# Local attention and RWKV channel mix: second query tile loaded and scored in halves, other load order, other product orders

## The chip, the cores and the metric

The kernel runs on one core of one Trainium2 chip. The metric is device time in microseconds: the median of three runs of the whole program. On a core, TensorE (PE) multiplies matrices, VectorE (DVE) and ScalarE (ACT) do the elementwise work, GpSimd (POOL) does a few small things here, and SyncE (SP) issues every DMA of this kernel.

## The reference

```python
# attention: q, k, v of shape (4, 8, 768, 64), 8 memory keys and values per head
for c in range(24):                       # chunks of 32 queries
    k_full = concat(mem_k, k[chunk with 16 to the left, 8 to the right])   # 64 keys
    v_full = concat(mem_v, v[the same])
    s = q[chunk] @ k_full.T / 8
    a = exp(s - max(s)); a = a / (sum(a) + 1e-9)
    out[chunk] = a @ v_full
x = out as (4, 768, 512)
# RWKV channel mix, d_model 512, d_ff 1024
x_prev = x one token earlier (zero at the start of a sequence)
xk = mu_k * x + (1 - mu_k) * x_prev;  xr = mu_r * x + (1 - mu_r) * x_prev
k = maximum(xk @ w_k, 0);  v = (k * k) @ w_v;  r = sigmoid(xr @ w_r)
y = r * v
```

All of it is float32.

## The kernel before

The 3072 tokens are 24 query tiles of 128, two of which make a unit of 256 tokens; twelve units pass through the kernel. For a unit, PE computes the scores (`s`, from one load `qk` for each tile that holds queries and keys together), DVE and ACT make the softmax in `e` (maximum, subtraction, exponential, sum, normalization), and PE multiplies with the values (`px`, from the load `vw`). In the first three units `e` is transposed by PE against the identity `id_sb` (`pt`) and copied to `aTz`. From the fourth unit on DVE transposes it in blocks (`eT`, L900), SP writes that to DRAM (`eD`, L907) and reads it back in four pieces as `aTz` (L911); the rows of `px` go to the columns of `xT` in the same way from the seventh unit on (`xD`, `xT`).

The channel mix of a unit is made of `ph` (first product), `kf` (its relu and square), `pr` (gate product), `sg_sb` (sigmoid) and the second product. For accuracy, operands are split into a high and a low part (`xh`/`xl`, `wk`/`wl`, `ah`/`al`), each product is three matmuls, and the second product of a unit is composed of seven partial products p1 to p7, which collect in the banks `accx` (p1, p2), `accy` (p6, p5, p3) and `accz` (p7, p4). The weights arrive as 64-bit words (`raw`) that ACT (L465) and DVE (a sign mask L470, then a join L474) turn into floats. Units 0 and 1 work while the weights still arrive and use plain float32 matmuls (`xf`, `w`).

A planner in Python lists all operations with costs and lays each on its engine. PE's order is written out by hand: `LEAD` for units 0 and 1 (s scores, t transposes, a attention times values, h first product, g gate, v second product), and for each later unit a list in `STAGES` (h0 to h3 parts of the first product, s or z the scores of two or three units ahead, a, b or x the `px` of one or two units ahead, g the gates of the next unit, p1 to p7 partial products). `LOADS` is the order of the first loads. SP's queue takes one DMA after the other, in the planner's order; an issue that waits holds up all behind it. The others' order follows from the planner's costs, with extra waits named in `FORCE`: "n" makes tile 0's normalization wait for tile 1's subtraction, "j" makes w0's join wait for tile 1's normalization. Warm matmuls, which multiply zeros, are placed in PE's gaps before the first `ph`, to keep its clock up; a row `warm 128x256` of the order is one float32 matmul, which shows as two records in the trace. Tile 0 of unit 0 is loaded and scored in two halves (`first_part`), tile 1 whole (`part`).

Of the kernel before, what the change touches and what calls it, by code (L numbers as in the profile page):

```python
# [16 lines left out]
P = 128  # L17
# [19 lines left out]
FORCE = "njt"  # L37
HALF = 2
LOADS = "q0a q0b q1 id w0 v0 v1 w1a w1b w2 w4 w3 q3 q2 w5 w6 v2 w7 w8 v3 q4 w9 q5"
LEAD = "s0.0.0 s0.0.1 s0.1 t0 t1 a0 a1 h0.0.0 h0.0.1 h0.1.0 h0.2.0 h0.3.0 s1.0 s1.1 h0.3.1 g0.0.0 h0.3.2 g0.1.0 h0.3.3 g0.0.1 t2 g0.1.1 a2 t3 v0.0.0 a3 v0.1.0 s2.0 v0.1.1 h1.0.0 h1.0.1 v0.0.1 h1.0.2 h1.0.3 h1.1.0 h1.1.1 h1.1.2 t4 t5 h1.1.3 a4 a5 g1.0 s3.0 g1.1 v1.0.0 v1.0.1 g2.0 v1.1.0 g2.1 v1.1.1"  # L40
STAGES = {
# [19 lines left out]
FETCH, FETCH_LEAD, FETCH_US, FETCH_AT, FETCH_FROM, FETCH_RATE = 256, 40, 4.9, 123, 2600, (0.0046, 0.0088)  # L61
# [49 lines left out]
class Plan:  # L111
# [22 lines left out]
    def place(self, o, free, held):  # L134
# [14 lines left out]
        for eng, cost, port in o.alts:  # L149
            t = max([free.get(eng, 0.7)] + [e + (SELF if g == eng else HOP)[eng if g == eng else g] for e, g in ready])  # L150
            if eng == "pe":
                cost, _ = self.fetched(t, cost, port)
# [7 lines left out]
    def fetched(self, t, cost, n):  # L160
# [46 lines left out]
    def told(self, done):  # L207
# [56 lines left out]
    def turn(self, goal, ease):  # L264
# [10 lines left out]
        while len(done) < len(self.ops):  # L275
# [69 lines left out]
def local_attention__then__channel_mix(  # L345
# [41 lines left out]
    nc.vector.memset(zero_sb, 0.0)  # L387
    nc.gpsimd.memset(aTz[0:64, 1], 0.0)
# [154 lines left out]
    NG = 2 * QPU * NPAIR  # L543

    def scores(u):
# [24 lines left out]
        def part(c, n, prev, first):  # L570
# [68 lines left out]
            if u == 0 and c == QPU - 1:  # L639
# [3 lines left out]
            return o_s, [o_n] * n  # L643

        def first_part():
            mx, sm, pt = Slot("sm"), Slot("sm"), {}
            R = NPAIR // 2

            def e4(b):
                return T["e", 0].rearrange("p (h c r) k -> p h c r k", h=2, c=QPU)[:, :, 0, R * b : R * (b + 1)]  # L650

            def s4(b, h=None):
                if b == 0:
                    return T["s", 0, h][:, : R * NK].rearrange("p (r k) -> p r k", k=NK)
                return T["s", 0, 2].rearrange("p (h g k) -> p h g k", h=2, k=NK)[:, :, :R]

            def f_s(b):
                if b == 0:
                    for h in range(2):
                        T["s", 0, h] = ps("m", f"s0_0_{h}")  # L660
                        nc.vector.memset(s4(0, h)[0:CHUNK, :, 0:LEFT], NEG)
                    T["s", 0, 2] = ps("s", "s0_0_2", QPU)
                    nc.vector.memset(s4(1)[0:CHUNK, :, :, 0:LEFT], NEG)
                for r in range(R):
                    for j in range(NJ):
                        for h in range(2):
                            q, k = operands(0, R * b + r, j, slice(64 * h, 64 * h + 64))
                            k0 = LEFT if j == 0 else 0
                            o = s4(b, h) if b == 0 else s4(b)[:, h]
                            nc.tensor.matmul(o[CHUNK * j : CHUNK * (j + 1), r, k0:], q, k[:, k0:], start=True, stop=True)  # L670
# [3 lines left out]

            def f_max(b):
                if b == 0:
                    pt["mx"] = sb("sm", [P, 2, NPAIR], "mx0_0")
                    for h in range(2):
                        nc.vector.reduce_max(mxs(0)[:, h], s4(0, h), axis=AX.X)
                else:  # L680
                    nc.vector.reduce_max(mxs(1), s4(1), axis=AX.X)

            def f_sub(b):
                if b == 0:
                    T["e", 0] = sb("e", [P, NG, NK], "e0")
                    for h in range(2):
                        m = mxs(0)[:, h].unsqueeze(2).to_broadcast([P, R, NK])
                        nc.vector.tensor_sub(e4(0)[:, h], s4(0, h), m)
                else:
                    nc.vector.tensor_sub(e4(1), s4(1), mxs(1).unsqueeze(3).to_broadcast([P, 2, R, NK]))  # L690

            def f_exp(b):
                nc.scalar.activation(e4(b), e4(b), AF.Exp, scale=SCALE)

            def f_sum(b):
                if b == 0:
# [1000 lines left out]
```

## Time and profile before

| | |
|---|---|
| median of 3 runs | 376.4 us (376.38 to 376.56) |
| the profiled execution | 376.67 us, span 374.9 us |
| PE busy | 367.7 us, 98% of the span |
| DVE busy | 322.7 us, 86% |
| ACT busy | 206.2 us, 55% |
| DMA | 64.78 MB, mean 173 GB/s |
| granted TensorE clock | 1.00 in every row shown here |

The span is the time from the first to the last instruction of the core; 1.8 us of the profiled execution lie around it. PE's share of the span is high all through, so a change of the time must come out of the few microseconds in which PE is idle, or out of the stretch before its first useful product.

### The profile page before, as it was taken

How to read it: one execution, taken by the hardware profiler on the slowest of the kernel's cores; microseconds unless marked ns; L12 is line 12 of the kernel's file. 1: busy time of each engine (PE TensorE's matmuls, PEld its weight loads, DVE VectorE, ACT ScalarE, POOL GpSimd, SP SyncE). 2: the span in 40 equal slices, each digit the busy share in tenths (PEclk: the TensorE clock that was granted, in tenths of full speed). 3: DMA queues.
4: the chain of work that ended last, by engine and by line, in shares of the span. 5: the costliest groups of instructions: out<-in, count | busy, mean ns of one | idle time of the engine just before them, and what ended most of it. 6: DMA issues, size and time to landing. Idle time of an engine off the chain costs nothing.

```text
span 374.9 us, 11497 instructions
## 1 busy us (share of the span) xinstructions
PE 367.7 (98%) x5084; PEld 339.6 (91%) x5084; DVE 322.7 (86%) x524; ACT 206.2 (55%) x307; POOL 2.4 (1%) x9
## 2 busy tenths in 40 slices
PE   7999999999999999999999999999999999999996
PEld 5886579988999999999999998999999999999996
DVE  3899999999999499989699997996998988788274
ACT  2797996954774386475068157238338244156260
POOL 2000000000000000000000000000000000000000
PEclk9999999999999999999999999999999999999999
DMA  7999981324701735556692485266343340400101
GB/s 287 403 417 409 389 309 71 113 87 140 274 39 72 262 120 179 215 165 240 246 278 93 153 288 179 64 220 230 127 154 115 112 169 2 143 30 0 58 1 58
DMA packets 24146, 64.78 MB, mean 173 GB/s; under 512 B 2720, under 2 KB 10784, under 8 KB 23712
## 3 DMA queue, kind: packets, MB, share of 16 engines
q1 hardware_dynamic: 24096, 64.04, 47.8%
q8 instruction: 40, 0.66, 0.7%
q14 instruction: 10, 0.08, 0.1%
HBM read 49.88 MB, written 14.16 MB: 171 GB/s over the span
## 4 chain that ended last, share of the span: by engine, by line
PE 82%; DMA 9%; DVE 5%; SPq 1%; issue 1%; ACT 0%; DVEq 0%
PE ph L1479 26%; PE pr L1368 14%; PE accy L1270 10%; PE accx L1270 7%; PE accz L1270 6%; PE pv L1581 4%; DMA raw<-in_w_k_dram 4%; PE s L588 4%; PE ph L1454 3%; PE px L771 3%; PE px L843 2%; PE pv L1568 2%; DMA qk<-in_qk_dram 2%; DMA aTz<-eD 1%; DMA xT<-xD 1%
## 5 line engine op out<-in xcount | busy, mean ns | idle before, releaser
L1479 PE MATMUL ph<-xh,wk 128*128 128x256 f32 x320 | 89.1, 278 | 0.0
L1479 PE MATMUL ph<-xh,wl 128*128 128x256 f32 x320 | 88.0, 275 | 0.0
L1479 PE MATMUL ph<-xl,wk 128*128 128x256 f32 x320 | 88.0, 275 | 0.0
L1498 ACT ACTIVATE kf<-ph 128x512 f32<-128x512 f32 x47 | 27.6, 596 | 88.7 <-PE ph L1479 88.4
L1479 PEld LDWEIGHTS ph<-xh,wk 128*128 128x128 f32 x320 | 61.4, 192 | 0.8
L1479 PEld LDWEIGHTS ph<-xh,wl 128*128 128x128 f32 x320 | 61.5, 192 | 0.0
L1479 PEld LDWEIGHTS ph<-xl,wk 128*128 128x128 f32 x320 | 61.4, 192 | 0.0
L1215 DVE TENSOR_TENSOR al<-kf,ah 128x512 fp32r<-128x512 f32 x50 | 33.6, 679 | 1.8 <-PE accz L1270 1.6
L1368 PE MATMUL pr<-wr,xh 128*128 128x512 f32 x88 | 34.1, 388 | 0.0
L1368 PE MATMUL pr<-wr,xl 128*128 128x512 f32 x88 | 33.4, 379 | 0.0
L1368 PE MATMUL pr<-wl,xh 128*128 128x512 f32 x88 | 33.4, 379 | 0.0
L397 ACT CAST ah<-kf 128x512 fp32r<-128x512 f32 x45 | 27.3, 620 | 9.7 <-DVE kf L1193 7.2
L1505 ACT ACTIVATE kf<-kf 128x512 f32<-128x512 f32 x45 | 28.1, 632 | 1.1
L1377 ACT ACTIVATE sg_sb<-pr 128x512 f32<-128x512 f32 x24 | 14.0, 597 | 20.5 <-PE pr L1368 20.3
L1270 PE MATMUL accx<-wv,ah 128*128 128x256 f32 x80 | 22.1, 276 | 0.0
L1270 PE MATMUL accx<-wv,al 128*128 128x256 f32 x80 | 22.0, 275 | 0.0
L1270 PE MATMUL accx<-wl,ah 128*128 128x256 f32 x80 | 22.0, 275 | 0.0
L588 PEld LDWEIGHTS s<-qk 64*32 64x32 f32 x1472 | 15.2, 105 | 4.0 <-issue 2.9
L1368 PEld LDWEIGHTS pr<-wr,xh 128*128 128x128 f32 x88 | 16.7, 189 | 2.5
L1368 PEld LDWEIGHTS pr<-wr,xl 128*128 128x128 f32 x88 | 16.6, 189 | 2.3
L1368 PEld LDWEIGHTS pr<-wl,xh 128*128 128x128 f32 x88 | 16.7, 189 | 1.9
L588 PE MATMUL s<-qk 64*32 64x64 f32 x1472 | 17.2, 225 | 1.1 <-DMA qk<-in_qk_dram 1.1
(165 smaller groups left out, 956.0 us busy)
## 6 DMA issues: line engine op xcount, KB each, us to landing
qk<-in_qk_dram SPq DMA_DIRECT2D x23, 768.0 KB, 6.1
vw<-in_vw_dram SPq DMA_DIRECT2D x24, 512.0 KB, 5.2
out_dram<-o SPq DMA_DIRECT2D x23, 256.0 KB, 2.4
eD<-eT SPq DMA_DIRECT2D x9, 512.0 KB, 2.7
aTz<-eD SPq DMA_DIRECT2D x36, 128.0 KB, 3.0
raw<-in_w_v_dram SPq DMA_DIRECT2D x4, 1024.0 KB, 10.2
raw<-in_w_k_dram SPq DMA_DIRECT2D x3, 1024.0 KB, 10.6
xD<-aTz SPq DMA_DIRECT2D x6, 512.0 KB, 2.6
```

What stands on the lines that cost most here:

```text
L397: e.copy(dst, src)
L588: nc.tensor.matmul(s5[CHUNK * j : CHUNK * (j + 1), h, d - c, r, :], *operands(ts[d], r, j, slice(64 * h, 64 * h + 64)), start=True, stop=True,
L771: nc.tensor.matmul(p3[64 * h : 64 * h + 64, 2 * g : 2 * g + 2, CHUNK * j : CHUNK * j + CHUNK], v[:, g, h, j, :], a[:, h, g, j, :], start=True,
L1215: nc.vector.tensor_sub(low(n), place[n](), T["ah", u, n].bitcast(F32))
L1270: nc.tensor.matmul(o, x, w, start=(n in fresh and c + i == 0), stop=(c == cs[-1] and i == 2), skip_group_check=True)
L1368: nc.tensor.matmul(pairs(p), x[:, place_of(u)[k], c * P : (c + 1) * P], woven(w), start=(k + n == 0), stop=(k == KT - 1 and n == 2),)
L1377: nc.scalar.activation(sg, p, AF.Sigmoid)
L1454: nc.tensor.matmul(pairs(T["ph", u, f][:, i * UTOK : (i + 1) * UTOK]), w[:, fc], x[:, :, k].rearrange("p t n -> p n t"), start=(i + k + n ...
L1479: nc.tensor.matmul(pairs(p[:, i * UTOK : (i + 1) * UTOK]), w[:, fc], x[:, :, place_of(u)[k]].rearrange("p t n -> p n t"), start=(k + n == ...
L1498: e.activation(part(), p, AF.Relu)
L1505: e.activation(q, q, AF.Square)
L1581: nc.tensor.matmul(pairs(p), x[:, tc_], woven(w), start=(f + n == 0), stop=(f == FT - 1 and n == 2),)
```

## The change

The second query tile's `qk` is loaded as two DMAs of 128x768, scored in two halves of 64 matmul calls in all, and its maximum, subtraction, exponential and sum are done by halves. Tile 0's second half of scores goes to two banks of its own. The first value tile `vw` and the first weight chunk w0 are loaded ahead of `id_sb` and `mu_sb`. Of `FORCE` only "t" is left, which keeps a copy on ACT. The lists in `LOADS`, `LEAD` and `STAGES` are other permutations, and the planner's constants for warm matmuls and for PE's instruction fetch are other numbers. The diff cut to its core:

```diff
-FORCE = "njt"
+FORCE = "t"
 HALF = 2
-LOADS = "q0a q0b q1 id w0 v0 v1 w1a w1b w2 w4 w3 q3 q2 w5 w6 v2 w7 w8 v3 q4 w9 q5"
...
+WARM = ((0.2, 1.1), (0.9, 0.3), (0.12, 0.43))
+FUSED, FUSED_US = (), 1.2
+LOADS = "q0a q0b q1a q1b v0 w0 id v1 w1a w1b w2 w4 w3 q2 q3 w5 w6 w7 w8 v2 w9 v3 q4 q5"
...
 STAGES = {
-    0: "z h0 h2 h3 h1 x g0 p1 p7 p6 p2 p5 g1 p3 p4",
...
-    5: "h1 z h0 h2 x h3 p1 g0 p7 p6 g1 p5 p2 p4 p3",
...
+    0: "z h0 h2 h1 h3 x g0 p1 p7 p6 p4 p5 p2 g1 p3",
...
+    5: "z h0 h1 h2 x h3 g0 p1 p7 p6 g1 p2 p5 p4 p3",
...
+        def first_part(t, prev):
...
+            def f_max(b):
+                if b == 0:
+                    pt["mx"] = sb("sm", [P, 2, NPAIR], f"mx0_{t}")
+                heads(b, lambda h, s: nc.vector.reduce_max(mxs(b)[:, h], s, axis=AX.X))
...
+            def f_exp(b):
+                if not fused:
+                    nc.scalar.activation(e4(b), e4(b), AF.Exp, scale=SCALE)
+                    return
...
-            if t == 0:
-                l.append([op(("dma", 1.05), lambda b=b: f_load(0, b), new=[x] * (b == 0), use=[x] * b, due=0.1 * b) for b in range(2)])
-                loads.update(q0a=l[0][0], q0b=l[0][1])
+            if u == 0:
+                l.append([op(("dma", 1.05), lambda b=b, t=t: f_load(t, b), new=[x] * (b == 0), use=[x] * b, due=0.2 * t + 0.1 * b) for b in range(2)])
+                loads.update({f"q{t}a": l[t][0], f"q{t}b": l[t][1]})
...
-                n = 0 if ("ph", 0, 0) in T else int((o.start - busy - 0.2) / (0.43 if busy else 1.1))
+                gap = o.start - busy
+                spare, each = WARM[0] if not busy else WARM[1] if gap > 2 else WARM[2]
+                n = 0 if ("ph", 0, 0) in T else int((gap - spare) / each)
```

What it moves on the engines, at the two places that matter here. First the start of the program on SP, the queue of loads. Before:

```order
L561 DMA qk_86<-in_qk_dram 128x768 x2
L561 DMA qk_134<-in_qk_dram 128x1536
L416 DMA id_sb<-in_ident_dram 128x128
L417 DMA mu_sb<-in_mu_dram 128x8
L445 DMA raw_187<-in_w_k_dram 128x1024
L745 DMA vw_210<-in_vw_dram 128x1024
L745 DMA vw_212<-in_vw_dram 128x1024
L445 DMA raw_214<-in_w_k_dram 128x512 x2
L445 DMA raw_250<-in_w_k_dram 128x1024
L447 DMA sg_sb<-in_w_r_dram 128x2x512
L445 DMA raw_335<-in_w_k_dram 128x1024
```

and of the changed kernel:

```order
L572 DMA qk_87<-in_qk_dram 128x768 x2
L572 DMA qk_138<-in_qk_dram 128x768 x2
L786 DMA vw_183<-in_vw_dram 128x1024
L457 DMA raw_185<-in_w_k_dram 128x1024
L428 DMA id_sb<-in_ident_dram 128x128
L429 DMA mu_sb<-in_mu_dram 128x8
L786 DMA vw_233<-in_vw_dram 128x1024
L457 DMA raw_236<-in_w_k_dram 128x512 x2
L457 DMA raw_318<-in_w_k_dram 128x1024
L459 DMA sg_sb<-in_w_r_dram 128x2x512
L457 DMA raw_345<-in_w_k_dram 128x1024
```

The first `vw` and the first `raw` (w0) now stand ahead of `id_sb` and `mu_sb`; up to the fourth `raw` of 128x1024 the same loads are in the queue. On PE the same start, from the last scores of tile 0 to the first `px`, before:

```order
L1639 MATMUL warm<-zero_sb 128x256 x3
L588 MATMUL s_1_148<-qk_134 32x64 x32
L1639 MATMUL warm<-zero_sb 128x256 x5
L751 MATMUL pt_199<-id_sb,e_136 128x128 x4
L1639 MATMUL warm<-zero_sb 128x256 x3
L751 MATMUL pt_223<-id_sb,e_136 128x128 x4
L771 MATMUL px_232<-aTz,vw_210 64x2x32 x16
L771 MATMUL px_258<-aTz,vw_212 64x2x32 x16
```

and of the changed kernel:

```order
L1682 MATMUL warm<-zero_sb 128x256
L677 MATMUL s_1_146<-qk_138 32x64 x16
L1682 MATMUL warm<-zero_sb 128x256
L677 MATMUL s_1_146<-qk_138 32x64 x16
L1682 MATMUL warm<-zero_sb 128x256 x9
L792 MATMUL pt_220<-id_sb,e_82 128x128 x4
L792 MATMUL pt_228<-id_sb,e_82 128x128 x4
L812 MATMUL px_243<-aTz,vw_183 64x2x32 x16
L812 MATMUL px_266<-aTz,vw_233 64x2x32 x16
```

Tile 1's scores stand in two parts with a warm matmul between, nine warm matmuls follow in place of five, and the three between the two transposes `pt` are gone.

The second place is the stage of unit 5 (o5, with unit 8's softmax e8), on DVE, from the normalization of e8 to its block transpose eT8, before:

```order
L622 TENSOR_TENSOR e8_2667<-e8_2667,sum8_0_2969 128x1024
L1312 TENSOR_TENSOR o5_1_2916<-accz5_2897,o5_1_2916 128x256
L1032 TENSOR_TENSOR xl6_0_3017<-df6_2669,xh6_0_2914 128x1024
L1335 TENSOR_TENSOR o5_1_2916<-o5_1_2916,sg_sb_78 128x512
L1312 TENSOR_TENSOR o5_0_2867<-accy5_2920,o5_0_2867 128x256
L1340 TENSOR_TENSOR o5_0_2867<-accx5_2853,sg_sb_78 128x256
L1342 TENSOR_TENSOR o5_0_2867<-o5_0_2867,sg_sb_78 128x256
L900 STREAM_TRANSPOSE eT8_3204<-e8_2667 128x1024
```

and of the changed kernel:

```order
L633 TENSOR_TENSOR e8_2676<-e8_2676,sum8_0_2931 128x1024
L1256 TENSOR_TENSOR al2_5_2935<-kf5_1_2758,ah3_5_2972 128x512
L1073 TENSOR_TENSOR xl6_0_2989<-df6_2707,xh6_0_2907 128x1024
L1381 TENSOR_TENSOR o5_0_2914<-accx5_2890,sg_sb_78 128x256
L1353 TENSOR_TENSOR o5_1_2937<-accy5_2939,o5_1_2937 128x256
L941 STREAM_TRANSPOSE eT8_3017<-e8_2676 128x1024
```

Between the two, four instructions stand in place of six; the sums of accz and of the last accy, and the gates of o5_1 and o5_0, have gone behind eT8. On SP at the same place, before:

```order
L1315 DMA out_0_dram<-o5_1_2916 128x512
L1315 DMA out_0_dram<-o5_0_2867 128x512
L907 DMA eD8_3206<-eT8_3204 128x1024
L561 DMA qk20_3212<-in_qk_dram 128x1536
L911 DMA aTz_79<-eD8_3206 32x4x256 x4
L561 DMA qk21_3297<-in_qk_dram 128x1536
```

and of the changed kernel:

```order
L948 DMA eD8_3033<-eT8_3017 128x1024
L1356 DMA out_0_dram<-o5_1_2937 128x512
L1356 DMA out_0_dram<-o5_0_2914 128x512
L952 DMA aTz_79<-eD8_3033 32x4x256 x4
L572 DMA qk20_3144<-in_qk_dram 128x1536
L572 DMA qk21_3179<-in_qk_dram 128x1536
```

The write eD8 has moved ahead of the two output stores, and the four reads aTz<-eD8 ahead of both loads of queries and keys.


## Rows read from the trace of the kernel before

**Rows 1.** The view of PE's waits: engine, line, what for; us, times, longest us.

```profile
PE px L843 <- DMA aTz<-eD: 1.2, 2, 0.6
```

**Rows 2.** Busy time of the engines by stretches: length, busy us (instructions), granted clock, DMA share, GB/s.

```profile
16.56:40.00 23.44, 23.33 (x232) 17.20 (x228) 22.71 (x33) 20.52 (x31) 0.00 (x0) 1.00 1.02 412
...
200.00:374.90 174.90, 170.53 (x2187) 164.75 (x2186) 144.09 (x248) 77.97 (x117) 0.00 (x0) 1.00 0.33 113
```

**Rows 3.** Timeline of PE around the stall: start us, duration us, engine, line, operation, tiles, count.

```profile
224.17 0.28 PE L1479 MATMUL ph<-xh,wl 128*128 128x256 f32 x1
...
227.28 0.48 PE L1368 MATMUL pr<-wr,xh 128*128 128x512 f32 x1
```

**Rows 4.** Timeline of PE at the same place one stage later.

```profile
254.16 0.28 PE L1479 MATMUL ph<-xh,wl 128*128 128x256 f32 x1
...
255.78 0.48 PE L1368 MATMUL pr<-wr,xh 128*128 128x512 f32 x1
```

**Rows 5.** Timeline of DVE, 207 to 219 us.

```profile
209.38 1.21 DVE L622 TENSOR_TENSOR e<-e,sum 128x1024 f32<-128x1024 f32 x1
...
212.36 0.68 DVE L1335 TENSOR_TENSOR o<-o,sg_sb 128x512 f32<-128x512 f32 x1
212.96 0.42 DVE L1312 TENSOR_TENSOR o<-accy,o 128x256 f32<-128x256 f32 x1
...
213.96 1.24 DVE L900 STREAM_TRANSPOSE eT<-e 128x1024 f32<-128x1024 f32 x1
```

**Rows 6.** Timeline of SP's queue, 205 to 227 us.

```profile
215.22 0.33 SPq L907 DMA_DIRECT2D eD<-eT  x1
215.60 0.45 SPq L561 DMA_DIRECT2D qk<-in_qk_dram  x1
218.12 2.88 SPq L911 DMA_DIRECT2D aTz<-eD  x4
```

**Rows 7.** DMA issues of the whole run: line by tiles, KB of each, median us to landing.

```profile
vw<-in_vw_dram SPq DMA_DIRECT2D x24, 512.0 KB, 5.2
...
eD<-eT SPq DMA_DIRECT2D x9, 512.0 KB, 2.7
...
raw<-in_w_k_dram SPq DMA_DIRECT2D x3, 1024.0 KB, 10.6
```

**Rows 8.** Timeline of PE at the start.

```profile
1.18 2.93 PE L1639 MATMUL warm<-zero_sb 128*128 128x256 f32 x6 [1.18 <-DVE zero_sb L387]
4.05 0.68 PE L670 MATMUL s<-qk 64*32 64x48 f32 x32
4.98 0.68 PE L670 MATMUL s<-qk 64*32 64x48 f32 x32 [0.25 <-DMA qk<-in_qk_dram]
...
8.64 0.85 PE L588 MATMUL s<-qk 64*32 64x64 f32 x64 [1.08 <-DMA qk<-in_qk_dram]
9.42 2.43 PE L1639 MATMUL warm<-zero_sb 128*128 128x256 f32 x10
...
13.55 0.66 PE L751 MATMUL pt<-id_sb,e 128*128 128x128 f32 x4
...
16.56 2.48 PE L1425 MATMUL ph<-xf,w 128*128 128x128 f32 x17
```

**Rows 9.** Timeline of ACT at the start.

```profile
14.25 1.17 ACT L397 COPY aTz<-pt 64x512 f32<-64x512 f32 x2
```

**Rows 10.** Timeline of DVE at the start.

```profile
13.41 0.69 DVE L470 TENSOR_SCALAR raw<-raw 128x1024 uint32<-128x1024 uint32 x1
14.26 1.23 DVE L474 SCALAR_TENSOR_TENSOR w<-w,raw 128x1024 uint32<-128x1024 uint32 x1
```

**Rows 11.** Timeline of SP's queue, 236 to 256 us.

```profile
242.72 0.34 SPq L907 DMA_DIRECT2D eD<-eT  x1
...
247.77 1.75 SPq L911 DMA_DIRECT2D aTz<-eD  x4
```

**Rows 12.** The tile aTz between 240 and 256 us.

```profile
DMA to landing us min/median/max: 2.6/3.0/4.1
```

More of the change, by code (lines that the diff above doesn't have):

```diff
@@ L151, in place @@
             if eng == "pe":
-                cost, _ = self.fetched(t, cost, port)
+                o.ready = max([0.0] + [e + HOP[g] for e, g in ready if g != "pe"])
+                cost, _ = self.fetched(t, cost, port, o.ready)
             elif port:
@@ L158, in place, with fetched @@
         return best
-    def fetched(self, t, cost, n):
+    def fetched(self, t, cost, n, ready):
         d = self.count - FETCH_FROM
@@ L216, in edge @@
             need[b] += 1
-        follows, prev, waits = {}, {}, {}
+        follows, prev, waits, opened = {}, {}, {}, {}
         for o in done:
@@ L225, in told @@
                     waits[o].update(d for d in h[-n].users if d is not o)
+                if s.tag in opened and opened[s.tag] is not o:
+                    edge(opened[s.tag], o)
+                opened[s.tag] = o
                 h.append(s)
@@ L291, in turn @@
                 o.lone, o.n = o.alts[0][1:]
-                cost, self.marks = self.fetched(t, o.lone, port)
+                cost, self.marks = self.fetched(t, o.lone, port, o.ready)
                 free[eng] = t + cost
@@ L642, in part @@
                         prior[y].deps.append(o)
[L643 to L670, printed above, removed]
-            def mxs(b):
-                return pt["mx"][:, :, R * b : R * (b + 1)]
[L675 to L696, printed above, removed]
-                    pt["sum"] = sb("sm", [P, 2, NPAIR], "sum0_0")
-                sm = pt["sum"]
-                nc.vector.reduce_sum(sm[:, :, R * b : R * (b + 1)], e4(b), axis=AX.X)
-                if b:
-                    nc.vector.tensor_scalar_add(sm, sm, 1e-9)
-                    nc.vector.reciprocal(sm, sm)
-            def f_norm():
-                e = grid(T["e", 0], 0, 1)
-                nc.vector.tensor_mul(e, e, pt["sum"].unsqueeze(3).to_broadcast([P, 2, NPAIR, NK]))
-            o_s = o_b = None
-            es_, banks = [], [[Slot("m"), Slot("m")], [Slot("s")]]
-            for b in range(2):
-                o_s = op(("pe", 0.45, 80 - 16 * b), lambda b=b: f_s(b), [l[0][b], o_s], new=sum(banks, []) if b == 0 else [], use=[qs[0]] + banks[b], due=due["s", 0, 0, b])
-                o_m = op(("dve", 0.36 if b else 0.5), lambda b=b: f_max(b), [o_s, o_b], new=[mx] * (b == 0), use=[mx] + banks[b])
-                o_b = op(("dve", 0.36 if b else 0.5), lambda b=b: f_sub(b), [o_m], new=[es] * (b == 0), use=[mx, es] + banks[b])
-                es_.append(op(("act", 0.36), lambda b=b: f_exp(b), [o_b], use=[es]))
-            o_u = op(("dve", 0.36), lambda: f_sum(0), es_[:1], new=[sm], use=[es])
-            o_u = op(("dve", 0.74), lambda: f_sum(1), [o_u, es_[1]], use=[es, sm])
-            prior.update(norm=op(("dve", 0.63, True), f_norm, [o_u], use=[es, sm]))
-            return o_s, [prior["norm"]]
@@ L720, in scores @@
+            else:
+                prior.update(norm=o_n)
+            return o_s, [o_n]
         qs = [Slot(big("q", t)) for t in ts]
@@ L731, in scores @@
         for c in range(0, QPU, step):
-            o_s, o_n = first_part() if u + c == 0 else part(c, step, o_s, u > 0)
+            o_s, o_n = first_part(c, o_s) if u == 0 else part(c, step, o_s, u > 0)
             done += o_n
@@ L796, in attention @@
         da = due.get(("a", t), 0.0)
-        lv = loads[f"v{t}"] = op(("dma", 1.35), f_loadv, new=[vs], lat=3.3 if u > 3 else DLAT)
+        lv = loads[f"v{t}"] = op(("dma", 2.05 if t == 1 else 1.35), f_loadv, new=[vs], lat=3.3 if u > 3 else DLAT + 0.3 * (t == 1))
         if u >= MOVED:
```

97 lines of the change are left out of this document (91 added, 6 removed), and 10 rows, old and new, of the table STAGES.

## Prediction

> **What bounds the kernel now.** I first read PE's share of the span, 98% in the table, and then asked where the rest is. The view of waits gives one entry of weight behind the start: `px` L843 waits 1.2 us for the DMA `aTz<-eD`, in two pieces [rows 1]. The table by stretches says how little else there is: from 16.56 to 40 us PE is busy for 23.33 of 23.44 us, while DVE has 22.71, so the first weights are worked through by a DVE that is nearly full [rows 2]. From 200 us to the end PE lacks 4.4 us, which are the wait above and the way out after the last matmul. So there are two places: the start, before the first `ph` at 16.56 us, and the stall near 225 us.
>
> The stall in starts of instructions: the last `ph` goes off at 224.17, the `pr` behind the `px` block at 227.28, 3.11 us later [rows 3]. One stage on, the same two are at 254.16 and 255.78, 1.62 us apart and without a wait [rows 4]. The stall costs 3.11 - 1.62 = **1.49 us**. Its cause lies ten microseconds earlier: DVE has normalized e8 at 209.38 + 1.21 = 210.6, but takes up its block transpose (L900) only at 213.96, behind six other instructions, one of which, the sum at 212.96, needs the last partial product [rows 5]. SP issues the write at 215.22, then a 768 KB load of queries and keys at 215.60, then from 218.12 to 221.0 the four reads of `aTz`, which share the DMA engines with that load [rows 6].
>
> At the start PE is paced by data: the scores of tile 1 begin at 8.64 after a wait of 1.08 us for `qk`, ten records of warm matmuls follow, the second transpose `pt` is at 13.55, and the first `ph` comes 3.01 us after that [rows 8].
>
> **The stall, term by term.** In the changed order the write eD8 is issued ahead of the two stores and the reads ahead of both `qk` loads, and eT8 no longer stands behind the sum that needs the last product. It can begin at 210.6 at the earliest; the latest is 213.0, where that sum stood. I take 211.5, for two reasons: four instructions are still left between, and against that unit 8's scores, with which the chain to e8 begins, stand one block `ph` earlier in the stage's list. Its own 1.24 [rows 5] gives the write at 212.8. A write of this kind lands after 2.7 us in the median [rows 7], and once took 247.77 - 242.72 = 5.0 us until the reads behind it went out [rows 11]: reads from 215.5 to 217.8. Four reads take 1.75 us to issue [rows 11], and the last lands up to 4.1 us later [rows 12]: 221.4 to 223.7 us. PE wants the first at 224.28 (224.17 and one step of 0.11). Even eT8 at 213.0 with the slow write only reaches 225.2, 0.9 late, and takes back 0.9 of the gain. I take the whole 1.49 as gone; the bounds are 0.6 and 1.49.
>
> **The start, term by term.** What ends the wait at 8.64 is the load of tile 1. Its half with the last bytes can't come before the same bytes now, if what delayed it is the path and not the size. Upper bound: as before, 8.5. Lower bound: the second half of tile 0 is there at 4.98 [rows 8], two halves are 0.79 MB, and the stretch after the start moved 412 GB/s [rows 2], so 4.98 + 1.9 = 6.9.
>
> - *Late load (8.5).* The second half of tile 1's scores is 0.85 / 2 = 0.42 long [rows 8] and ends at 9.06. Nine warm matmuls are 18 records; ten took 2.43 with the tail of the last [rows 8], 0.216 from start to start, so 3.9 us, and the first `pt` is at 12.95. The second follows its four matmuls, at most the 0.66 of such a row [rows 8] later, at some 13.5 (before 13.55). `id_sb` must be there: behind the 512 KB `vw` and the 1024 KB `raw` [rows 7], 1.57 MB at 412 GB/s after 8.5 make 12.3, with its own small size 12.5; it is hidden by the warm matmuls, with 0.4 us to spare. ACT: PE's first transposes took 0.70 from start to the copy behind them (13.55 to 14.25 [rows 8, 9]), so 13.65, one copy 0.58 and two copies 1.17 [rows 9], end 15.40 (before 15.42): nothing. DVE gets a copy that ACT had: 0.58 to 0.7, from ACT's price and the next wider instructions of DVE; from 13.65 it runs to 14.3, and w0's mask and join, from 13.41 to 15.49 before [rows 10], follow: 2.08 us, to 16.4, against 15.49. The two instructions that PE needs after the join (the mixing on ACT and DVE) began at 15.45 before, so part of the 0.9 was slack. PE's first `ph` came 1.07 after the join's end; if all of that is needed, it comes at 17.4, +0.9; if it needs only the last 0.35 or so, at 16.75, +0.2. I take **+0.2**, since `xf` waits for `px`, whose copies are no later, and keep +0.9 as the bound.
> - *Early load (6.9).* Scores end at 7.4, the warm matmuls at 11.3, `id_sb` is there at 6.9 + 3.8 + 0.2 = 10.9; everything is 1.65 us earlier, the first `ph` at 15.0. The weights behind (the same bytes) don't come earlier, and DVE, 22.71 of 23.44 us busy, has to work them off, so not all of it stays. Half a unit's scores now stand ahead of the last first-product block and fill part of the wait. Bounds 0.5 and 1.6, I take **1.1 us** kept.
>
> What decides between them is whether tile 1's load was late for its size or for its path. The two halves of tile 0 were used 0.93 us apart [rows 8]; tile 1, of twice the size, took 8.64 - 4.98 = 3.7 us, twice the 1.9 of the rate. So something held it up there, and since the bytes ahead of it and its own are unchanged, I give the late case more weight.
>
> A rule speaks against halving. The second half of tile 0 was there 0.93 us behind the start on the first [rows 8], in which 0.39 MB pass at 412 GB/s, so these two halves show no latency between them. A rule speaks against halving: the Trainium skill (DMA: Bandwidth & Descriptors, Rules for kernel authors) asks for loads of 1 MiB or more, and the same page gives a fixed cost of about 2.0 us for each DMA. By it, if both halves paid in turn, the sum would be an estimated 377.1, rival F below; tile 0's rows speak for the other.
>
> **The rest.** The moved products of units 6 to 8 put the gate of the second half (0.68, and a sum of 0.42 [rows 5]) ahead of the block transpose and take two sums of 0.42 from ahead of it: net +0.3, up to +0.8 where the sums had only waited. The tightest of these is unit 9's, transposed in stage 6 and used in stage 7: its reads are issued from 247.77 to 249.52 [rows 11], the last lands at most 4.1 us later, by 253.6 [rows 12], and its `px` is wanted at 254.27 [rows 4]; 0.7 us of slack at least, so nothing. Some DVE and ACT casts change engines for nothing on average; where DVE is full (16.56 to 40 us) each extra 0.7 us could cost as much. I take 0, bounds -0.3 and +0.7.
>
> **Sum.** The profiled execution took 376.67, 0.27 above the median of 376.4; terms read from it are taken off the median. Late load: 376.4 - 1.49 + 0.2 + 0 = 375.1. Early load: 376.4 - 1.49 - 1.1 = 373.8.
>
> **Rivals.** *A, late load, stall gone*: 375.1 (chance 0.45). *B, early load, stall gone*: 373.8 (0.26). *C, the stall moves*: unit 9's `px` or a product waits 0.5 to 1 us for its operands; for it, the slack of 0.7 us there and a DVE without idle time; against it, that those waits are absent now [rows 1]. 376.4 - 1.49 + 0.2 + 0.8 = 375.9 (0.14). *D, the change doesn't do it*: eT8 comes at its latest, the write is slow, and the reads are 0.9 late: 376.0 with the late load (0.04). *E, slower: the clock.* The first six warm records took 2.93 us, 0.43 apart, half of full pace; after tile 0 they ran at 0.22 [rows 8]. In the changed order fewer warm matmuls lie between tile 0 and tile 1, and if PE is at the lower level when the nine begin, 18 records at 0.43 take 7.7 us instead of 3.9 and hold up `pt`: +3.8 at most, 376.4 - 1.49 + 0.2 + 3.8 = 378.9; it decides from 1.5 us of delay on, that is from some seven of the 18 records at half pace. Against it: a wait of 1.08 us before tile 1 didn't cost the level before, and the work of tile 0 before which it rose is still there (0.07). The Trainium skill (TensorE: Matmul & The Clock Gate, Part 1) has the half rate as the default that activity lifts, and the trace has both paces. *F, the second half pays a latency of its own*: a write of 0.52 MB takes 2.7 us [rows 7], 1.3 of it at 412 GB/s, so 1.4 are latency; `pt` and `ph` come so much later than in A, 376.5 (0.04).
>
> **Range and chances.** A measurement of this kernel tells about 0.2%, 0.75 us: faster is under 375.65, slower over 377.15. A and B are faster but for a tail of A (0.05); C, D and F are the same for the most part, 0.04 of them faster and 0.01 slower; E is slower. That makes 0.71 faster, 0.21 same, 0.08 slower. The range takes in the bounds of A (374.8 to 376.0 with a part of the stall left) and B (373.3 to 374.4) and most of C: 373.3 to 376.2. A alone would be 374.7 to 375.9.
>
> **What would show it.** Stall: `px` of unit 8 starts 0.2 us after the last `ph`, no wait for `aTz<-eD` is left, and eT8 starts near 211.5. Start: `pt` at 12.95 and `ph` at 16.6 to 16.8 (A) or 11.3 and 15 (B); the time of tile 1's second scores tells which. Wrong would be: warm records 0.43 apart behind tile 1, `pt` waiting for `id_sb`, a DVE join of w0 that ends after 16.5, or new waits of `px` or of the products in units 6 to 8.

## The result and the profile after

The changed kernel took 378.21 us in the median of 18 runs (376.28 to 381.52), the kernel before 376.44 in the 18 beside them; the ratio is 1.0063 with the interval 1.0046 to 1.0080. It is slower by some 2 us, where 1.3 us faster was forecast, and lies outside the forecast range of 373.3 to 376.2. The profiled execution took 379.67 us, its span is 377.9.

The view of PE's waits in the changed kernel shows that the wait of `px` for `aTz<-eD` [rows 1] is gone, and what has come:

```profile
PE px L812 <- issue: 1.3, 1, 1.3
...
PE pt L792 <- DMA id_sb<-in_ident_dram: 0.7, 1, 0.7
PE s L599 <- issue: 0.6, 1, 0.6
PE ph L1520 <- issue: 0.4, 1, 0.4
PE accy L1311 <- DVE o L1353: 0.4, 1, 0.4
```

The first two are at the start, the last three behind 186 us. PE's timeline at the start, with the columns of [rows 8]:

```profile
7.31 0.46 PE L677 MATMUL s<-qk 64*32 64x64 f32 x32
7.70 4.15 PE L1682 MATMUL warm<-zero_sb 128*128 128x256 f32 x18
12.56 1.06 PE L792 MATMUL pt<-id_sb,e 128*128 128x128 f32 x8 [0.71 <-DMA id_sb<-in_ident_dram]
14.94 3.59 PE L812 MATMUL px<-aTz,vw 128*64 128x64 f32 x64 [1.32 <-issue]
18.46 1.72 PE L1466 MATMUL ph<-xf,w 128*128 128x128 f32 x13
```

The first row is the second half of tile 1's scores. The eighteen warm records run at 0.22 us, as forecast. Then PE stands idle until `id_sb` is there, 0.71 us, makes both transposes in a row, and is idle for another 1.32 us. The 64 records of `px` take 3.59 us, and the first `ph` comes at 18.46 against 16.56. Busy time by stretches shows that the slow `px` goes with a lower clock (the granted clock is the number ahead of the DMA share):

```profile
12.00:14.00 2.00, 1.06 (x8) 0.86 (x8) 0.75 (x2) 1.71 (x3) 0.24 (x2) 1.00 1.02 414
14.00:15.00 1.00, 0.06 (x2) 0.09 (x3) 0.84 (x2) 0.96 (x3) 0.00 (x0) 0.94 1.15 483
15.00:16.00 1.00, 1.00 (x20) 1.00 (x22) 0.97 (x2) 0.32 (x1) 0.00 (x0) 0.50 0.94 397
```

From 10 to 12 us PE was busy for 1.85 of 2 us at a granted clock of 1.00; from 12 to 15 it was busy for 1.12 of 3, and from 15 the clock is at 0.50, which is 1.2 GHz; it stays there to 18 us and is 0.85 in the microsecond behind. ACT and DVE at the same place:

```profile
12.27 1.25 ACT L477 ACTIVATE w<-raw 128x512 f32<-128x512 f32 x2 [1.13 <-DMA raw<-in_w_k_dram]
13.54 1.78 ACT L409 COPY aTz<-pt 64x512 f32<-64x512 f32 x3
```

```profile
12.09 0.69 DVE L734 TENSOR_TENSOR e<-e,sum 128x512 f32<-128x512 f32 x1
14.16 0.68 DVE L411 COPY aTz<-pt 64x512 f32<-64x512 f32 x1 [1.38 <-ACT aTz L409]
```

ACT waits for w0, not for `pt`, then converts both halves of it, and only then makes the copies of `pt`; DVE's copy waits for ACT's first one. It ends at 14.16 + 0.68 = 14.84, and `px` starts 0.10 us later, as it does in E1 and E4: what the view puts down to issue reads as a wait for this copy. So `px` stands 2.38 us behind the first `pt`.

Near 225 us, on DVE, SP and PE, each from its timeline:

```profile
213.79 1.23 DVE L941 STREAM_TRANSPOSE eT<-e 128x1024 f32<-128x1024 f32 x1
```

```profile
215.04 0.34 SPq L948 DMA_DIRECT2D eD<-eT  x1
...
218.11 2.22 SPq L952 DMA_DIRECT2D aTz<-eD  x4
220.43 0.85 SPq L572 DMA_DIRECT2D qk<-in_qk_dram  x2
```

```profile
228.35 0.28 PE L1520 MATMUL ph<-xh,wl 128*128 128x256 f32 x1
228.56 1.48 PE L884 MATMUL px<-vw,aTz 64*32 64x64 f32 x128
```

The reads go out ahead of the loads, and `px` of unit 8 starts 0.21 us behind the last `ph`. This part came as forecast.

### The profile page after: what moved, and what is told of

Its sections match the earlier page's. It is cut to its first block, busy times and chain, and to the rows that moved or that the text cites. A ratio compares the mean times of both kernels' runs of the same rounds, so it can differ in the third digit from the quotient of the medians.

```text
span 377.9 us, 11509 instructions
## 1 busy us (share of the span) xinstructions
PE 369.8 (98%) x5086; PEld 340.7 (90%) x5086; DVE 322.4 (85%) x527; ACT 208.3 (55%) x311; POOL 2.5 (1%) x9
## 3 DMA queue, kind: packets, MB, share of 16 engines
HBM read 49.88 MB, written 14.16 MB: 169 GB/s over the span
## 4 chain that ended last, share of the span: by engine, by line
PE 86%; DVE 6%; DMA 4%; issue 2%; SPq 1%; ACT 0%; DVEq 0%
PE ph L1520 26%; PE pr L1409 14%; PE accy L1311 10%; PE accz L1311 6%; PE accx L1311 6%; PE s L599 4%; PE pv L1622 4%; PE px L812 4%; PE ph L1466 3%; PE ph L1495 3%; DMA id_sb<-in_ident_dram 2%; PE pv L1609 2%; PE px L884 2%; DMA xT<-xD 1%; DVE al L1256 1%
## 5 line engine op out<-in xcount | busy, mean ns | idle before, releaser
L1539 ACT ACTIVATE kf<-ph 128x512 f32<-128x512 f32 x48 | 28.4, 596 | 76.7 <-PE ph L1520 74.7
L409 ACT CAST ah<-kf 128x512 fp32r<-128x512 f32 x47 | 29.1, 622 | 18.9 <-DVE kf L1234 9.7
L1546 ACT ACTIVATE kf<-kf 128x512 f32<-128x512 f32 x47 | 29.4, 630 | 1.3
L1311 PE MATMUL accx<-wl,ah 128*128 128x256 f32 x80 | 22.0, 275 | 0.0
L1311 PE MATMUL accx<-wv,al 128*128 128x256 f32 x80 | 22.0, 275 | 0.0
L1311 PE MATMUL accx<-wv,ah 128*128 128x256 f32 x80 | 22.0, 275 | 0.0
```

The source lines that it names most:

```text
L409: e.copy(dst, src)
L1311: nc.tensor.matmul(o, x, w, start=(n in fresh and c + i == 0), stop=(c == cs[-1] and i == 2), skip_group_check=True)
L1539: e.activation(part(), p, AF.Relu)
L1546: e.activation(q, q, AF.Square)
```

## The experiments

Each kernel ran on a chip beside the kernel before, whose median was 375.81 us in the first group (E1 to E4), 375.85 in the second (E5 to E8) and 375.68 in the third (E9 to E12). Two things vary between executions of one kernel, and the comparisons below have to allow for them.

- *The start.* The first profile, with the first `ph` at 16.56, was of a start later than most: in E3, E6, E7, E9 and E10, whose start is the same program, it comes between 14.88 and 15.75. What varies is when the load of tile 1 is there: its scores begin at 8.64 in the first profile and between 6.96 and 7.83 in these five. From these scores to the first `ph` it is 7.92 to 7.95 us in all six. So starts are compared from the start of tile 1's last scores on.
- *The end.* The last store of the output lands 1.7 us after its issue in twelve of the fourteen profiles, and 2.9 and 3.0 us in those of E5 and E7.

The difference of two medians and the one that the ratio gives are up to half a microsecond apart (E6: 1.26 and 0.8), and the intervals are some 0.2% to each side. So differences of a few tenths of a microsecond say nothing.

**E1, the changed kernel again.** No edit.

> The changed kernel once more, for a second profile. Theory S (start and instruction supply): first ph again at 17 us or later, since the transposes pt wait for id_sb near 12.4 us and the copies behind them leave PE idle before px; whether the granted clock falls to 0.5 there differs between executions. On PE two waits put down to issue, 0.4 us and more, near 187 and 220 us, at the same places of the program. Time 377 to 380 us. Rival O (the later orders alone): the start is the same to 0.3 us as before, and the loss stands behind 60 us in waits for DVE.

Measured: 378.65 us (377.88 to 379.58), ratio 1.0074 (1.0046 to 1.0102). PE's waits:

```profile
PE px L812 <- issue: 1.3, 1, 1.3
...
PE pt L792 <- DMA id_sb<-in_ident_dram: 0.8, 1, 0.8
...
PE ph L1520 <- issue: 0.3, 1, 0.3
```

The start is the same, with a granted clock of 0.50 between 16 and 19 us; the first `ph` is at 19.37. The wait near 187 us is not there this time; the one at 220 is.

**E2, `id_sb` ahead.**

```diff
-LOADS = "q0a q0b q1a q1b v0 w0 id v1 w1a w1b w2 w4 w3 q2 q3 w5 w6 w7 w8 v2 w9 v3 q4 q5"
+LOADS = "q0a q0b q1a q1b id v0 w0 v1 w1a w1b w2 w4 w3 q2 q3 w5 w6 w7 w8 v2 w9 v3 q4 q5"
```

> The changed kernel with id_sb and mu_sb ahead of the first value tile and w0 in the queue of loads, as before the change. Theory S: no wait for id_sb is left, pt starts by 9.5 us, first ph near 15.5 us, granted clock 1.00 at the start; 1.5 to 3 us faster than the changed kernel, 375 to 376.5 us. Rival O: no gain over 0.3 us, 378 us.

Measured: 377.06 us (376.11 to 379.9), ratio 1.0041 (1.0020 to 1.0061); 1.6 us faster than E1, but still 1.2 us slower than the kernel before. PE's timeline:

```profile
12.99 0.63 PE L792 MATMUL pt<-id_sb,e 128*128 128x128 f32 x4 [0.52 <-DVE e L734]
...
15.20 1.15 PE L812 MATMUL px<-aTz,vw 128*64 128x64 f32 x32 [0.49 <-ACT aTz L409]
16.28 8.05 PE L1466 MATMUL ph<-xf,w 128*128 128x128 f32 x50
```

The clock holds (32 records of `px` take 1.15 us, as in E6 and E7), but the second `pt` now waits 0.52 us for DVE's normalization of tile 1, so the start is not at the 15.5 us that I expected, and the time is above the 375 to 376.5 that I gave. Rival O falls all the same.

**E3, the kernel before with the new orders of stages** (the whole table `STAGES` of the change, of which the diff in the section on the change shows two rows).

> The kernel before with the later units' orders (STAGES) of the changed kernel; loads and start as before. Theory S: first ph at 16.6 us, the px stall of 1.5 us near 225 us is gone; what of it is given back depends on where the instruction blocks of 256 end: with no wait for issue 374.9 us, with both of the changed kernel 376.3 us; the wait of accy for DVE stays (0.4 us). Rival O: 377.5 us or more, as the changed kernel.

Measured: 376.90 us (376.15 to 379.32), ratio 1.0042 (1.0022 to 1.0061): 1.1 us slower than before, though no `px` waits near 225 us:

```profile
PE accy L1270 <- DVE o L1312: 0.5, 2, 0.3
PE accx L1270 <- DVE al L1215: 0.4, 1, 0.4
```

No wait for issue is left; three products wait for DVE in its place (at 107, 120 and 211 us). This lies between my two theories: the loss behind 60 us is real without the changed start, and it isn't instruction supply.

**E4, the changed kernel with the old orders of stages** (the table of before).

> The changed kernel with the later units' orders (STAGES) of the kernel before; loads and start changed. Theory S: first ph at 17 us or later as in the changed kernel, px stall near 225 us of about 1.5 us back, no wait of accy for DVE; 376.8 to 378.5 us. Rival O: as the kernel before, 376.4 us.

Measured: 378.35 us (376.35 to 379.82), ratio 1.0065 (1.0040 to 1.0090). The profile has the first `px` at 15.61 after an idle 1.31 us, its 64 records in 3.61 us and the first `ph` at 19.15, and the old wait of `px` L884 for `aTz<-eD` (0.9 us). So the start alone makes the kernel slower by 2.5 us.

**E5, PE kept busy ahead of `px`.**

```diff
+FILL = 3
...
         def f_a():
+            if t == 0:
+                for _ in range(FILL):
+                    nc.tensor.matmul(T["warm"][:, : 2 * P], zero_sb[:, :P], zero_sb, start=True, stop=True)
             if u < MOVED:
...
-                    warm = warm or ps("m", "warm")
+                    warm = T["warm"] = warm or ps("m", "warm")
```

> The changed kernel with three more warm matmuls (six records, 1.3 us) on PE between the second pt and the first px, where it stands idle for 1.3 us. Theory C (idle PE lowers the clock): granted clock 1.00 through the start, 64 records of px in 2.0 us in place of 3.6, first ph near 17 to 17.8 us; 1 us or more faster than the changed kernel in the median, 377.5 us or less. Rival W (the clock falls for another reason, as the load of the chip): px at 0.50 as before, no gain.

Measured: 378.19 us (377.38 to 379.22), ratio 1.0065 (1.0044 to 1.0085). PE's timeline and the clock:

```profile
13.14 1.06 PE L793 MATMUL pt<-id_sb,e 128*128 128x128 f32 x8 [0.70 <-DMA id_sb<-in_ident_dram]
14.04 1.46 PE L805 MATMUL warm<-zero_sb 128*128 128x256 f32 x6
15.51 2.08 PE L816 MATMUL px<-aTz,vw 128*64 128x64 f32 x64
17.59 2.05 PE L1470 MATMUL ph<-xf,w 128*128 128x128 f32 x16
```

```profile
14.00:16.00 2.00, 1.99 (x25) 1.52 (x25) 1.28 (x2) 1.82 (x4) 0.00 (x0) 1.00 1.04 434
```

With the gap filled the clock is at 1.00 and 64 records of `px` take 2.08 us. Theory C holds for the mechanism, and Rival W falls. In the median I missed: E5 is 0.5 us under E1, within its spread, and level with the 18 runs of the changed kernel, where I expected 1 us or more. Not every execution falls to the lower level: of those 18 runs 4 had a mean granted clock of 0.996 or less, which some 3 us at half clock make; their median is 379.8 us, that of the other 14 is 378.0. E1 had 2 such runs of 4, E5 none of 6. So the clock costs 1.8 us in a run in which it falls, but only 0.2 us of the median of 18: even without it the changed kernel is slower than the kernel before.

**E6, one swap in SP's queue of the kernel before.**

```diff
     for x, y in zip(first, first[1:]):
         y.behind = (x,)
+    loads["q20"].behind = loads["q21"].behind = (moved[8][0][-1],)
```

> The kernel before with one swap in SP's queue: the load qk20 stands behind the four reads aTz<-eD8 in place of ahead of them; every other instruction is in the same order. Theory S: the px stall of 1.5 us near 225 us is gone or under 0.3 us, no new wait comes, since no other order changes; 1.2 to 1.5 us faster than before, 374.3 to 374.6 us. Rival G (what is gained there is lost again to the next wait, as DVE or the supply of instructions is no faster): within 0.4 us of before.

Measured: **374.59 us** (374.29 to 376.04), ratio 0.9979 (0.9965 to 0.9994): 1.26 us faster than before. SP's queue now, against [rows 6]:

```profile
214.42 0.33 SPq L907 DMA_DIRECT2D eD<-eT  x1
217.32 1.88 SPq L911 DMA_DIRECT2D aTz<-eD  x4
219.30 0.85 SPq L561 DMA_DIRECT2D qk<-in_qk_dram  x2
```

In both kernels the reads go out 2.9 us behind the write (218.12 - 215.22 and 217.32 - 214.42). What changed is how long they take, from issue to landing, by the view of the tile `aTz` in the kernel before (217 to 224 us) and in E6 (216 to 224 us):

```profile
DMA to landing us min/median/max: 5.3/6.2/6.4
```

```profile
DMA to landing us min/median/max: 2.7/2.9/2.9
```

So the stall came not from a late issue of the reads; they were slowed by the 768 KB load that went out ahead of them. PE has no wait over 0.3 us behind the start. Theory S holds. The gain is 1.26 us by the medians and 0.8 by the ratio, with 0.2 to 1.3 as its interval; that it is more than Rival G's 0.4 us is likely, and the missing wait speaks for it. E6 and E7 are the two versions that come out ahead of both kernels.

**E7, the new order of stage 5 alone, in the kernel before.**

```diff
-    5: "h1 z h0 h2 x h3 p1 g0 p7 p6 g1 p5 p2 p4 p3",
+    5: "z h0 h1 h2 x h3 g0 p1 p7 p6 g1 p2 p5 p4 p3",
```

> The kernel before with the changed order of stage 5 alone. Theory S: px stall gone, and of it the wait of accy for DVE near 211 us (0.4 us) and a wait for issue of up to 0.8 us are given back: 375 to 375.6 us, 0.2 to 0.8 us faster than before. Rival O: slower than before, as with all new orders.

Measured: **374.67 us** (374.39 to 375.68), ratio 0.9980 (0.9963 to 0.9997): 1.18 us faster by the medians, 0.8 by the ratio. Besides the first warm matmul's wait for its zeros, which every run has, these are all of PE's waits:

```profile
PE s L670 <- DMA qk<-in_qk_dram: 0.3, 1, 0.3
PE px L771 <- ACT aTz L397: 0.2, 1, 0.2
```

Nothing was given back, and the gain is larger than the 0.2 to 0.8 us that I gave: neither the wait of `accy` near 211 us nor one for issue, which I had expected of this order, is there. They belong to its company, not to it.

**E8, `id_sb` ahead and the old orders of stages** (both edits, E2 and E4): what is left of the change is tile 1's halves, the order of units 0 and 1, the dropped waits "n" and "j", the constants for warm matmuls, and the order of the other loads.

> The changed kernel with id_sb ahead again and the later units' orders of before: what is left of the change is the halves and the order of units 0 and 1. Theory S: first ph at 16.3 us as with id_sb ahead, since the second pt waits for DVE, px stall of 1.5 us back: 376 to 376.8 us, no faster than before. Rival H (the halves alone bring the start forward): first ph by 15 us, 374.5 us.

Measured: 376.92 us (375.40 to 378.32), ratio 1.0025 (1.0007 to 1.0044): 1.1 us slower than before, just above what I gave; Rival H falls. The first `ph` is at 16.55, 8.57 us behind tile 1's last scores (7.98), 0.65 us more than in the kernel before. The second `pt` waits for DVE, and the old wait of `px` for `aTz<-eD` is back with 1.2 us:

```profile
PE pt L792 <- DVE e L734: 0.5, 1, 0.5
```

**E9, the new orders of stages 2, 3 and 4 alone, and E10, those of stages 6 to 11 alone**, in the kernel before. Edits: rows 2, 3 and 4 of the changed table; rows 0, 10 and 11 of it.

> The kernel before with the changed orders of stages 2, 3 and 4 alone. All new orders together cost 1.1 us and stage 5 alone gained 1.2, so stages 2 to 4 and stages 6 to 11 must lose some 2.3 us together. Theory S (the loss sits in products that wait for DVE): waits of accx for DVE near 107 us (0.5 us) and of accy near 120 us (0.35 us) as with all new orders, px stall near 225 us still there: 376.3 to 377 us, 0.5 to 1.2 us slower than before. Rival L (the loss sits in units 6 to 11): within 0.3 us of before.

> The kernel before with the changed orders of stages 6 to 11 alone (the default row and rows 10 and 11). Theory S: px stall near 225 us still there, no other wait of PE over 0.3 us, within 0.5 us of before. Rival L: 1 us or more slower than before, with waits of px or of products behind 230 us.

Measured: E9 382.32 us (381.53 to 382.64), ratio 1.0174 (1.0147 to 1.0201); E10 376.08 (374.80 to 377.15), ratio 1.0010 (0.9992 to 1.0028), not told apart from before. E10 came as Theory S had it. E9 has the two waits that Theory S named, but its time is 5 us over the range. PE's waits of E9:

```profile
PE px L843 <- issue: 3.8, 1, 3.8
...
PE accx L1270 <- DVE al L1215: 0.4, 1, 0.4
```

The wait of `accy` at 120 us is too short for this view; its first matmul starts 0.42 us behind the one ahead of it, where 0.11 is the usual step. E9's loss of 6.6 us is larger than that of all new orders together, by one wait of 3.8 us at 197 us, which E3 doesn't have, and by what follows it: the granted clock is at 0.50 from 196 to 202.8 us, which costs up to half of these 6.8 us more.

```profile
198.00:199.00 1.00, 1.00 (x94) 1.00 (x81) 1.00 (x4) 0.99 (x2) 0.00 (x0) 0.50 0.12 25
```

Put down to issue, the wait ends 0.1 us behind DVE's subtraction that frees the bank of unit 8's scores:

```profile
195.99 1.22 DVE L606 TENSOR_TENSOR e<-s,mx 128x1024 f32<-128x1024 f32 x1
```

In the kernel's text `px` and the scores take their banks from the same pool (`ps("s", ...)`); that this bank is what `px` waited for is still my reading, which no run tests. Parts of the table can't be costed one by one and added: the planner lays DVE's work by the whole of it. What stands is that the two small waits, `accx` at 107 and `accy` at 120 us, come with rows 2 to 4, and that the rows for stages 6 to 11 cost nothing that can be measured (at most 1.1 us by the interval).

**E11, the halves alone, and E12, the halves with both copies of the first `pt` on ACT.** E11 is the changed code with `FORCE`, `LEAD` and `STAGES` of before and its `LOADS` with q1 in two (in `LEAD`, s0.1 becomes s0.1.0 s0.1.1), so it keeps the changed constants for warm matmuls; E12 adds the last line.

```diff
-FORCE = "t"
+FORCE = "njt"
-LOADS = "q0a q0b q1a q1b v0 w0 id v1 w1a w1b w2 w4 w3 q2 q3 w5 w6 w7 w8 v2 w9 v3 q4 q5"
+LOADS = "q0a q0b q1a q1b id w0 v0 v1 w1a w1b w2 w4 w3 q3 q2 w5 w6 v2 w7 w8 v3 q4 w9 q5"
...
-        by = [("act", 0.5)] if t == 1 and "t" in FORCE else either(act=(0.5,), dve=(0.61,))
+        by = [("act", 0.5)] if t <= 1 and "t" in FORCE else either(act=(0.5,), dve=(0.61,))
```

> The kernel before with tile 1 loaded, scored and made softmax of in halves and nothing else of the change (order of loads, of units 0 and 1 and of stages, and the waits njt as before). Theory D (the halves make DVE's chain longer, by instructions of 0.42 where one of 0.69 stood, and by its copy of pt): the second scores come no later than the whole ones, first ph still 0.3 to 1 us later than in the kernel before (15.5 to 15.8 us in its last profiles), time 376.2 to 376.9 us. Rival H (the loss of the start lies in the order of units 0 and 1 and of the loads): first ph by 15.5 us, no slower than before.

> The run with the halves alone, with both copies of the first pt on ACT, so that DVE has none. Theory D: DVE's copy waited for ACT's and DVE's normalization and the join of w0 stood behind it, so first ph is 0.3 to 0.6 us earlier than with the halves alone. Rival H: the same to 0.2 us, or later as ACT now has four copies in a row.

Measured: E11 383.43 us (382.94 to 384.04), ratio 1.0207 (1.0180 to 1.0234); E12 378.82 (378.18 to 379.29), ratio 1.0083 (1.0061 to 1.0105). E11's total is far over the range that I gave. Both totals are spoiled by waits behind the start that the planner's other layout brought: `accy` L1311 waits for DVE for 3.3 us at 124 us in E11, behind which the granted clock is at 0.50 from 124.5 to 127.9 us, and for 0.9 us at 122 us in E12, where a `pt` at 39 us also waits 1.0 us for DVE. The start can still be read. From tile 1's last scores to the first `ph`, in E11 and in E12:

```profile
7.48 0.45 PE L677 MATMUL s<-qk 64*32 64x64 f32 x32
...
11.71 0.63 PE L792 MATMUL pt<-id_sb,e 128*128 128x128 f32 x4 [0.56 <-DVE e L734]
...
16.77 7.40 PE L1466 MATMUL ph<-xf,w 128*128 128x128 f32 x47
```

```profile
8.25 0.45 PE L677 MATMUL s<-qk 64*32 64x64 f32 x32
...
12.48 0.63 PE L792 MATMUL pt<-id_sb,e 128*128 128x128 f32 x4 [0.56 <-DVE e L734]
...
16.84 7.49 PE L1466 MATMUL ph<-xf,w 128*128 128x128 f32 x47
```

From these scores the first `pt` stands 4.23 us behind in both runs, the first `ph` 9.29 us in E11 and 8.59 in E12, against 7.92 in the kernel before. So the halves lengthen the start by 0.7 us, and DVE's copy in E11 by another 0.7. Theory D holds for the start in both parts; the first `ph` of E12 is no earlier in the span only because its scores came 0.77 us later. The rows on DVE, E11's copy and normalization of tile 1 first:

```profile
12.38 0.68 DVE L411 COPY aTz<-pt 64x512 f32<-64x512 f32 x1
12.99 0.67 DVE L734 TENSOR_TENSOR e<-e,sum 128x512 f32<-128x512 f32 x1
```

The normalizations of tile 0 and of tile 1 in E12:

```profile
11.55 0.68 DVE L734 TENSOR_TENSOR e<-e,sum 128x512 f32<-128x512 f32 x1
...
13.03 0.69 DVE L734 TENSOR_TENSOR e<-e,sum 128x512 f32<-128x512 f32 x1
```

And that of tile 1 in the kernel before:

```profile
12.81 0.69 DVE L622 TENSOR_TENSOR e<-e,sum 128x512 f32<-128x512 f32 x1
```

The chain on DVE from the start of tile 1's last scores to the end of its normalization is 4.86 us before (8.64 to 12.81 + 0.69; E6 and E7 have 4.87 and 4.86), 5.47 in E12 (8.25 to 13.03 + 0.69) and 6.18 in E11 (7.48 to 12.99 + 0.67), where the copy stands in it. In the changed kernel it is 5.47 (7.31 to 12.09 + 0.69), since the copy comes behind it there. The first tile's normalization, for which the first `pt` waits in E11 and E12, stands behind tile 1's halves.

## Why the prediction was wrong

**The stall: right in its mechanism, the size at the upper end.** The working gave 1.49 us with bounds 0.6 and 1.49; the two kernels that remove it and keep the rest gained 1.26 (E6) and 1.18 (E7) by the medians, 0.8 by the ratios. eT8 started at 213.79 in the profile where I had 211.5; the start alone is 1.9 us later there, and the wait at 187 us lies ahead of it. The reads were in time. One step of the working wasn't needed: I had the late eT8 as part of the cause, but E6 removes the stall with eT8 behind the same six instructions as before, by moving one load.

**The start: the step that failed first.** My term was +0.2 us with the load late or a gain of 1.1 with it early, both against a first `ph` at 16.56. In both cases the working has the first `ph` 8.0 to 8.1 us behind tile 1's last scores (16.75 - 8.64, and 15.0 - 6.98), about as in the kernel before (7.92). Measured are 11.15 us in the changed kernel and 11.1 to 11.3 in E4 and E1. The missing 3 us are 5.25 in place of 4.3 to the first `pt`, 2.38 in place of 1.4 from there to `px`, and 3.52 in place of 2.4 from `px` to `ph`. So this term was too small by some 3 us in an execution in which the clock falls, and by 1.6 in E5 (9.69 us), where it doesn't. In medians of whole runs, single changes on the same chip give: halves, order of units 0 and 1 and what else is left in E8, 376.92 - 375.85 = +1.1 us; the first value tile and w0 ahead of `id_sb`, 378.35 - 376.92 = +1.4 us (E4 against E8, of two groups). With the new orders of stages the second of these is 378.65 - 377.06 = +1.6 us (E1 against E2). Three parts of the working fell:

- *"it is hidden by the warm matmuls, with 0.4 us to spare"* held only if tile 1 is late. Tile 1's scores came early (second half at 7.31), as in my case B, but `id_sb` did not follow at 10.9: its `pt` was released at 12.56. I had taken the loads behind tile 1 to arrive one after the other at 412 GB/s. The rate was right: from 7.3 to 12.5 us the DMA engines moved 411 GB/s, 2.1 MB. But the first value tile, w0 and `id_sb` are 1.64 MB, part of which had come before; the rest of what was moved belongs to loads behind them in the queue, which share the engines with them. The same is to be seen on tile 1 in the kernel before, which landed late while the engines moved 381 GB/s (6.5 to 8.6 us). So in these rows a load's place in the queue alone doesn't say when it lands.
- *One copy and two copies of ACT, from 13.65.* I had ACT free at the end of the first `pt`. It had just begun on both halves of w0, which landed 0.2 us ahead of `id_sb` (conversions from 12.27 to 13.5), and DVE's copy, which I ran beside ACT's, waited for it. `px` came 2.38 us behind the first `pt`, where I had 1.4.
- *The clock.* Rival E had the mechanism and the wrong place: I priced half pace for warm matmuls behind tile 1 and looked for its cause ahead of them. They ran at full pace; `px` fell behind them, after 0.71 and 1.32 us of idle PE that the order has no warm matmuls for. The price is 3.59 - 2.08 = 1.5 us of `px` in an execution that falls (E5), and as only some do, 0.2 us of the median. The Trainium skill (TensorE: Matmul & The Clock Gate, Part 1) has the half rate as the state after idleness. The traces bear it out: the clock fell behind 1.9 us of idle PE in 3 us here, and at waits of 3.8 us in E9 and 3.3 us in E11.

The halves themselves I had counted as nothing but a chance of earlier scores. They cost DVE 0.6 us more from the scores to the normalization, and hold up tile 0's (E12: 3.3 us behind the scores of tile 1; before, at 10.86, 2.2 us). That brings the first `ph` 0.7 us later from the scores on (E12), and where DVE also copies `pt` ahead of the normalization, 1.4 us (E11).

The latency of its own for the second half, weighed as rival F, did not show: with halves tile 1's last scores start at 7.3 to 8.3 us (eight profiles), the whole tile's at 7.0 to 8.6 (six). So neither a gain nor a loss of load time came with the halves that stands out from this spread.

**The rest: mis-sized.** I took 0 with bounds -0.3 and +0.7 for the other moved work. All new orders on the old start cost +1.1 us in place of the -1.2 of stage 5 alone (E3, E7), so 2.3 us are lost there; 1.3 us of it are the waits of `accx` and `accy` for DVE, counted from start to start (0.9 us in the view). In the two profiles the difference is smaller: from the first `ph` to the start of the last matmul 355.2 us in E3 and 353.3 in E7, 1.9 us, so that 0.6 us stay without a name in the rows. With the changed start the orders cost only 378.65 - 378.35 = 0.3 us (E1, E4), and 377.06 - 376.92 = 0.1 us with `id_sb` ahead (E2, E8), both within the noise; why the loss is larger on the old start, no run shows. I had looked for the slack of one `px`; it was the slack of products to DVE that went, in stages that I had not looked at.

The three differences, +1.1, +1.4 and +0.3, lead from the kernel before by way of E8 and E4 to E1, so they make up E1's distance by construction and are no proof of each other; the second one alone was measured twice. What stays open is the split of the +1.1 of E8: 0.65 us are the longer start, which is what E12 shows for the halves, and the rest is within the noise. The share of the order of units 0 and 1 was not measured by itself.

## What to carry to other kernels

A stall that a queue causes can be removed in the queue: one load moved behind four reads gained about 1 us here (1.26 by the medians, 0.8 by the ratio), while the new orders gained the same at that place and lost 2.3 us elsewhere. When a load is moved ahead of another, ask what the one behind it releases, and whether TensorE is idle until then; idle TensorE ahead of dense work can cost twice, once for the wait and once for the lower clock (in E9 3.8 us and up to 3.4 us more). Read a start from the event that varies between executions, here tile 1's scores, and not from the beginning of the span: read from the span, E12 seemed to show that a copy costs nothing that costs 0.7 us. Splitting a short chain in halves lengthens it where each instruction has a fixed part (0.42 against 0.69 us here for half the width).

## What the runs showed of the hardware

- A granted clock of 1.00 fell to 0.50 after 3 us in which PE was busy for 1.12 us, with no single gap over 1.5 us; it came back after some 3 us of dense `px`. It is so in all three profiles of this start (the changed kernel, E1, E4), but only in 8 of their 30 runs, by the mean granted clock.
- Some waits put down to issue look as if PE waited for its own instructions; no run tests this. Those that end at 187.3 and 220.4 us of the changed kernel stand at instructions 5313 and 6337 of PE, counted in the trace with weight loads and sequencer, 1024 apart; E1's and a short one of E2, which the view puts down to PE itself, at 6337, one of E4 at 5825. All five are multiples of 256 apart, and instructions come in 39 packets of 16 KB for some 10,260 of PE's. In the changed kernel both waits ended 2.4 us after the start of such a packet. The same program had the first wait in one execution and not in another. The Trainium skill (Runtime: NRT & Kernel Launch, Instruction fetch mechanics) gives blocks of 256 instructions and calls the cost of a boundary mostly hidden; here the largest of these waits was 0.6 us, where dense `s` ran over one.
- ACT's and DVE's copies of the two halves of `pt` ran one behind the other in every run that had both: DVE waited for ACT in most (1.38 us in the changed kernel, which contains ACT's own delay, 0.54 in E8), ACT for DVE in E11 (0.67 us). On which rule of the program or the chip, no run shows.
- A read of 128 KB landed in 2.7 to 2.9 us with no load ahead of it and in 5.3 to 6.4 us behind a load of 768 KB issued 2.5 us earlier (E6 and the kernel before).
- The last store landed 1.7 us after its issue in twelve profiles and 2.9 to 3.0 in two. The twelve runs of E7 fall in two groups, 374.4 to 374.7 and 375.4 to 375.7 us; its profile, with the late store, is of the upper one. That this store makes the groups in other runs too can't be seen without their profiles.
